# A fused attention and MLP kernel: output tiles stored as two half tiles, one slot apart

## The chip, the cores and the metric

The kernel runs on one core of a Trainium2 chip. The metric is the device time of one launch in microseconds (us). The kernel before was run three times: 504.86, 505.30 and 510.37 us, median 505.3.

## What is computed

Attention over 8 batches, 8 heads, 576 positions and head width 64, in which all scores further than tau = 0.02 below the row's maximum are dropped, followed by a two-layer network on all 4608 tokens:

```python
scores = scale * np.matmul(q, k.transpose(0, 1, 3, 2))
thresh = np.max(scores, axis=-1, keepdims=True) - tau
scores = np.where(scores >= thresh, scores, -1000000000.0)
attn = np.exp(scores - max) / (sum + 1e-09)          # row-wise
x = (attn @ v), heads side by side                    # 4608 x 512
h = x @ w_in                                          # 4608 x 2048
out = (h - np.tanh(h)) @ w_out                        # 4608 x 512
```

## The kernel before

The order of all work is written out by hand. One loop (line 852) runs over slots `s`; a slot is one score tile of 128 queries by 576 keys, and nine slots are a pair of heads. There are 288 score tiles. In each slot the program emits, in this order: the scores of a tile eight slots ahead (TensorE), their reduction to `sc` and a row maximum (VectorE, line 420), the thresholding `z` of a tile (`kink`, ScalarE, line 447), a transpose of `z`, the exponential `pT` (ScalarE), a piece of the network, finished stores, the product with v, and preparation of later pairs.

Transposes: for the first six pairs TensorE transposes `z`. For the rest `kink` issues one DMA transpose per two tiles on SyncE's queue (SP, line 454), `zT<-z`, and ScalarE's exponential (line 483) reads `zT`. `q` and `k` of the later pairs, split into two 16-bit parts on GpSimd (POOL, lines 228 to 232), are transposed by DMA on the same queue (`kT<-khl`, `qT<-qhl`, line 315); GpSimd then writes `kS` from `kT` (line 337), which TensorE needs for the scores (lines 401 and 410).

The loads of q, k and v of later pairs are issued on ScalarE's queue (`load_part`, line 175).

The network: batch after batch is taken up as a "stage" of 512 tokens as soon as its attention is done. `hidden` makes 16 tiles of 128 by 512 (psH, line 579), `bend` and `shrink` make tanh and the difference `g` (lines 592 and 598), and `project` (line 603) makes four output tiles of 128 rows by 512, each of four parts of four matmuls (psY, line 605). A stage is spread over 32 or 36 slots by a pattern of letters (`PATTERN`), so an output tile is finished every 8 to 10 slots. Stages 0 to 7 are the first 512 tokens of each batch, stage 8 the 64 left over of all batches. What is not done when the slots end runs afterwards.

An output tile is copied from PSUM to `yo` (`y_pool`, two buffers; line 617 on VectorE, or 615 on ScalarE in the tail). Its store is not issued at once: `project` appends a function to `stores`, and the slot loop runs what waits in `going` and then moves all of `stores` but the newest into `going`. So a tile's store is issued in the slot after that in which the next tile is finished. It is issued on SP, in SP's order between the transposes. The rows of a tile lie four apart in the output, 2 KB each. After the slots, all stores are issued as soon as they exist. Stage 8 stores 64 rows at a time (line 626).

Of the kernel before, what the change touches and what calls it, by code (L numbers as in the profile page):

```python
# [18 lines left out]
def kernel(  # L19
# [11 lines left out]
    nc = tc.nc  # L31
    P = 128
# [307 lines left out]
    def turn_first(t, part):  # L340

        hl = hls[0, t[0]]
        c0, c1 = ((0, 5), (5, TPP))[part]
        pl, tag = (ps_y, "y") if t == "ks" else (ps_h, "h")
        ps = pl.tile([P, 5 * P], FP16, name=f"ps1_{t}", tag=tag)
        for c in range(c0, c1):
            o = ps[:, (c - c0) * P : (c - c0 + 1) * P]
            if t == "ks":
                for a in range(2):
                    turn_chunk(o[64 * a : 64 * a + 64, :], c, hl[:, c, 1 - a, :])  # L350
            else:
                turn_chunk(o, c, hl[:, c, :, :].rearrange("p a d -> p (a d)"))
        if part == 0:
            mats[0, t] = qk_tile(t)
        dst, n = mats[0, t][:, c0 * P : c1 * P], (c1 - c0) * P
        if part == 1 or t == "q":
            nc.scalar.copy(out=dst, in_=ps[:, 0:n])
        else:
            nc.vector.tensor_copy(out=dst, in_=ps[:, 0:n])
# [17 lines left out]
    def kind(i):  # L377

        return "AB"[i % 2]

    def place(i):

        p, j = divmod(i, TPP)
        j = j - p % 2
        return (p, None, 4) if j in (-1, 8) else (p, j // 4, j % 4)

    def scores(i):
        p, hh, t = place(i)
        qT, kT, kS = mats[p, "q"], mats[p, "k"], mats[p, "ks"]
        ps = ps_big.tile([P, 1024], F32, name="psS", tag="big")  # L390
        main, rem, lo = slice(0, 512), slice(512, 576), 0
        if kind(i) == "B":
            main, rem, lo = slice(512, 1024), slice(448, 512), 448
        if hh is None:
            qrem = REM
            if q_by_dma(p):
                qrem = (slice(512, 640, 2), slice(513, 640, 2))
            for n, kk in enumerate((kT, kS)):
                for dst, cols in ((main, main_keys), (rem, rem_keys)):
                    for hh in range(2):  # L400
                        nc.tensor.matmul(  # L401
                            out=ps[64 * hh : 64 * hh + 64, dst],
                            lhsT=qT[:, qrem[hh]], rhs=cols(p, kk, hh),
                            start=(n == 0), stop=(n == 1),
                        )
        else:
            lhs = qT[:, (5 * hh + t) * P : (5 * hh + t + 1) * P]
            for n, kk in enumerate((kT, kS)):
                for dst, cols in ((main, main_keys), (rem, rem_keys)):
                    nc.tensor.matmul(  # L410
                        out=ps[:, dst], lhsT=lhs, rhs=cols(p, kk, hh),
                        start=(n == 0), stop=(n == 1),
                    )
        sc = sc_pool.tile([P, S], F32, name="sc")
        if kind(i) == "B":
            mx = mxs[i] = mxs.pop(i - 1)
        else:
            mx = mxs[i] = mx3[i // 2 % len(mx3)]
        c = int(kind(i) == "B")
        nc.vector.tensor_scalar(  # L420
            out=sc, in0=ps[:, lo : lo + S], scalar1=SC, scalar2=None,
            op0=ALU.mult, op1=ALU.max, accum_out=mx[:, c : c + 1],
        )
        scs[i] = sc

    def shift(i):

        if kind(i) == "A":
            return
        mx = mxs.pop(i)  # L430
        nb = st_pool.tile([P, 9], F32, name="nb", tag="nb")
        nc.vector.tensor_scalar(  # L432
            out=nb.rearrange("p (a b) -> p a b", b=3)[:, :, 0:2],
            in0=mx.rearrange("p (a b) -> p a b", b=4)[:, :, 0:3],
            scalar1=-1.0, scalar2=tau, op0=ALU.mult, op1=ALU.add,
        )
        nbs[i - 1], nbs[i] = nb[:, 0:1], nb[:, 1:2]
# [135 lines left out]
    gs, stores = {}, []  # L573
# [29 lines left out]
    def project(m, ms, part, ps, last, cols=slice(0, d_model)):  # L603
        for n in range(4 * part, 4 * part + 4):
            nc.tensor.matmul(  # L605
                out=ps, lhsT=gs[m][:, n, ms * P : (ms + 1) * P],
                rhs=w_out_sb[:, n, cols], start=(n == 0), stop=(n == DF_C - 1),
            )
        if part == 3:
            nc_ = cols.stop - cols.start  # L610

            pl, tag = (y_pool, "yo") if nc_ == d_model else (t_pool, "th")
            yo = pl.tile([P, d_model], F32, name="yo", tag=tag)[:, 0:nc_]
            if last:
                nc.scalar.copy(out=yo, in_=ps)
            else:
                nc.vector.tensor_copy(out=yo, in_=ps)  # L617
            if m < B:
                rows = out[m * S : m * S + MB, :].rearrange("(p c) n -> c p n", c=4)
                stores.append(lambda: nc.sync.dma_start(out=rows[ms], in_=yo))  # L620
            else:
                for h in range(2):
                    b = 2 * ms + h
                    eng = nc.scalar if h and nc_ < d_model else nc.sync
                    stores.append(
                        lambda b=b, h=h, eng=eng: eng.dma_start(
                            out=out[b * S + MB : (b + 1) * S, cols],
                            in_=yo[64 * h : 64 * h + 64, :],
                        )
                    )  # L630


    EARLY = lambda m: 3 if m else 3
# [150 lines left out]
    for p in range(DUAL, NPAIR):  # L784
        first = TPP * p - AHEAD
        at = lambda d, f: plan.setdefault(first - d, []).append(f)
# [45 lines left out]

    todo, stage = [], 0

    going = []
    fold = const.tile([P, 64], BF16, name="fold")

    for at in sorted(plan):
# [7 lines left out]
    for i in range(NTILE + 3):  # L846
        at = i - SOONER[min(i // TPP, 6)]
# [4 lines left out]
    for s in range(-AHEAD, NTILE + LAG + 3):  # L852
        p, j = divmod(max(s, 0), TPP)
        if 0 <= s < NTILE and j == 2 + LAG and p % HPAIR == 0 and p >= HPAIR:
            assert not todo
            todo = [(s + i, step) for i, step in layers(stage, False, PATTERN(stage))]
            stage += 1
        if s == NTILE:
            todo = [(s + n, step) for n, step in enumerate(layers(stage, True))]
            stage += 1  # L860
        if 0 <= s + AHEAD - 1 < NTILE:
            shift(s + AHEAD - 1)

        n = s + AHEAD
        if 0 < n < NTILE and place(n)[1] is None and kind(n) == "B":
            scores(n - 1)
        if 0 <= n < NTILE and (place(n)[1] is not None or kind(n) == "B"):
            scores(n)
        if s == 1 - AHEAD:
            for t in ("k", "q", "ks"):  # L870
                turn_first(t, 1)
        for i in kinks.pop(s, []):
            kink(i)
        bend()
        for i in wts.pop(s, []):
            weights(i)
        while todo and todo[0][0] <= s < NTILE + FIRST:
            todo.pop(0)[1]()
        if s == 0:
            nc.vector.tensor_tensor(  # L880
                out=fold, in0=ident_bf[:, 0:64], in1=ident_bf[:, 64:P], op=ALU.add
            )
        shrink()
        for store in going:
            store()
        going = stores[:-1]
        del stores[:-1]
        for i in atts.pop(s, []):
            pp, jj = divmod(i, TPP)
            if i < NTILE:  # L890
                attend(i)
                odd = pp % 2
                if jj == 3 + odd:
                    norm(pp, 0)
                elif odd and jj in (0, 8):
                    norm(pp - (jj == 0), 1)
            if pp and jj == 1 + pp % 2:
                emit_x(pp - 1)
        for step in plan.pop(s, []):
            step()  # L900
        for _ in range(cast_when.count(s + AHEAD)):
            w_cast()
        for _ in range(load_when.count(s + AHEAD)):
            w_load(next(pieces))

    for store in going:
        store()
    for _, step in todo:
        step()
        bend()  # L910
        shrink()
        for store in stores:
            store()
        stores.clear()
    while stage < NMB:
        for step in layers(stage, True):
            step()
            bend()
            shrink()
            for store in stores:  # L920
                store()
            stores.clear()
        stage += 1
# [37 lines left out]
```

## Time and profile before

| what | value |
|---|---|
| median of three runs | 505.3 us |
| profiled execution: time, span of its instructions | 511.6 us, 509.7 us |
| output tiles stored whole on SP (line 620) | 32, of 256 KB; median 3.8 us from issue to landing |
| `zT<-z` transposes on SP | 117, median 4.7 us to landing |
| `kT<-khl`, `qT<-qhl` transposes on SP | 23 and 24, median 5.2 and 4.3 us |
| 64-row stores of stage 8 (line 626) | 6 of 128 KB and 2 of 64 KB on SP, 2 of 64 KB on ScalarE's queue |

The profiled execution took 6.3 us longer than the median of the runs. Engines are PE (TensorE matmuls), PEld (its weight loads), DVE (VectorE), ACT (ScalarE), POOL (GpSimd) and SP (SyncE); a "q" behind a name means the engine's instruction queue. Issuing a DMA takes time on the queue that issues it; landing is when its data is confirmed written. In a row of slices each digit is a fortieth of the span, 9 meaning 90% or more. A line of waits reads: who waited, for what, us in total, how often, the longest. In the view of one line, the three numbers with slashes are the minimum, median and maximum duration in ns.

### The profile page before, as it was taken

Reading aid. Unit: us, or ns where it says so; the run is one execution under the profiler, and the core shown is the slowest. Engines: PE = TensorE matmul, PEld = TensorE weight load, DVE = VectorE, ACT = ScalarE, POOL = GpSimd, SP = SyncE. Lnnn points to the kernel's source line nnn. Section 1 sums busy time; section 2 is a strip of 40 time slices with the busy share of each in tenths; the row PEclk is TensorE's granted clock in tenths of the full one; section 3 lists DMA queues with packets and bytes.
Section 4 is the critical chain, followed back from the end, with each engine's and each line's share of the span. In section 5 each row is a group of like instructions: output and inputs, shape, how many; then the busy total and the mean of one; then the engine's idle time right before and its main releaser. Section 6 shows DMA issues by size and latency. Waiting matters only on the chain.

```text
span 509.7 us, 12184 instructions
## 1 busy us (share of the span) xinstructions
PE 484.8 (95%) x4283; PEld 270.9 (53%) x4345; DVE 400.2 (79%) x1150; ACT 431.7 (85%) x617; POOL 291.4 (57%) x390
## 2 busy tenths in 40 slices
PE   8999899889999989999999999999998999999997
PEld 4666566445555545555555555555554555544444
DVE  5899978878889879988898789889886887544440
ACT  5999998889999889999999999899979999533430
POOL 8999999886765375757675666569456700000000
PEclk9999999989999999999999999999999999999999
DMA  7852658999999999999999999999999986311013
GB/s 206 262 155 89 195 190 220 159 225 214 231 217 245 192 254 209 238 241 242 242 195 221 261 238 225 207 242 240 213 191 258 187 144 115 87 41 42 23 41 82
DMA packets 233341, 95.32 MB, mean 187 GB/s; under 512 B 203968, under 2 KB 222656, under 8 KB 233280
## 3 DMA queue, kind: packets, MB, share of 16 engines
q1 hardware_dynamic: 212336, 72.87, 75.1%
q10 hardware_dynamic: 20944, 21.67, 16.1%
q8 instruction: 34, 0.56, 0.5%
q14 instruction: 27, 0.22, 0.2%
HBM read 36.70 MB, written 9.44 MB: 91 GB/s over the span
## 4 chain that ended last, share of the span: by engine, by line
PE 57%; POOL 12%; DMA 9%; issue 7%; ACT 7%; DVE 5%; ACTq 1%; SPq 0%; POOLq 0%; DVEq 0%
PE psY L605 18%; PE psH L579 14%; PE psS L410 13%; DMA zT<-z 6%; PE psO L513 3%; POOL kS L337 3%; PE psHt L579 3%; ACT pT L483 3%; DMA vraw<-in_v_dram 3%; ACT z L447 2%; DVE g L598 2%; POOL qhl L232 2%; DVE sc L420 2%; PE psS L401 2%; ACTq L175 1%
## 5 line engine op out<-in xcount | busy, mean ns | idle before, releaser
L420 DVE TENSOR_SCALAR_CACHE_REDUCE sc<-psS 128x576 f32<-128x576 f32 x288 | 213.5, 752 | 27.1 <-PE psS L410 12.9
L447 ACT ACTIVATE z<-sc,nb 128x576 bf16<-128x576 f32 x288 | 216.1, 770 | 8.0 <-DVE nb L432 5.7
L483 ACT ACTIVATE pT<-zT 128x1152 f16<-128x1152 bf16 x117 | 135.2, 1155 | 12.3 <-DMA zT<-z 10.6
L605 PE MATMUL psY<-w_out_sb,g 128*128 128x512 bf16 (+1 forms) x564 | 140.8, 373 | 1.6 <-issue 0.2
L579 PE MATMUL psH<-xT,w_in_sb 128*128 128x512 bf16 x448 | 119.4, 381 | 5.1 <-issue 2.0
L337 POOL COPY kS<-kT 64x1152 f16<-64x1152 f16 x62 | 70.8, 1142 | 86.3 <-DMA kT<-khl 72.7
L598 DVE SCALAR_TENSOR_TENSOR g<-th,psH 128x512 bf16<-128x512 f32 x128 | 87.6, 685 | 33.6 <-ACT th L592 32.9
L410 PE MATMUL psS<-kT,qT 128*128 128x512 f16 (+1 forms) x512 | 104.7, 286 | 4.1 <-DVE sc L420 1.9
L410 PE MATMUL psS<-kS,qT 128*128 128x512 f16 (+1 forms) x512 | 105.1, 287 | 0.0
L410 PEld LDWEIGHTS <-qT 128*128 128x128 f16 x1024 | 72.5, 98 | 59.0 <-issue 3.8
L592 ACT ACTIVATE th<-psH 128x512 f32<-128x512 f32 x128 | 74.6, 583 | 21.4 <-PE psH L579 21.4
L605 PEld LDWEIGHTS <-g 128*128 128x128 bf16 x592 | 51.1, 98 | 54.6 <-DVE g L598 0.4
L579 PEld LDWEIGHTS <-w_in_sb 128*128 128x128 bf16 x576 | 49.4, 98 | 57.4 <-issue 6.3
L513 PE MATMUL psO<-vb,pT 128*128 128x65 bf16 x1024 | 53.3, 194 | 0.0
L513 PEld LDWEIGHTS <-pT 128*128 128x128 f16 x1024 | 44.2, 98 | 9.6
L232 POOL TENSOR_TENSOR qhl<-qraw,qhl 128x576 f16<-128x576 f32 x31 | 39.7, 1281 | 2.6
L232 POOL TENSOR_TENSOR khl<-kraw,khl 128x576 f16<-128x576 f32 x31 | 39.7, 1280 | 2.7
L475 ACT ACTIVATE pT<-psZ 128x512 f16<-128x512 bf16 (+1 forms) x54 | 35.1, 654 | 2.4 <-PE psZ L466 2.1
L506 PE MATMUL psO<-vb,pT 128*128 128x130 bf16 x128 | 28.2, 220 | 3.7 <-ACT pT L483 3.6
L617 DVE COPY yo<-psY 128x512 f32<-128x512 f32 (+1 forms) x31 | 21.1, 680 | 13.1 <-PE psY L605 12.4
L539 DVE TENSOR_TENSOR osb<-psO,rc 128x256 bf16<-128x256 f32 x64 | 27.2, 424 | 2.2
L228 POOL TENSOR_SCALAR qraw<-qraw 128x576 f32<-128x576 f32 x31 | 20.8, 671 | 11.1 <-DMA qraw<-in_q_dram 10.8
(77 smaller groups left out, 452.1 us busy)
## 6 DMA issues: line engine op xcount, KB each, us to landing
out_dram<-yo SPq DMA_DIRECT2D x32, 256.0 KB, 3.8
kraw<-in_k_dram ACTq DMA_DIRECT2D x24, 288.0 KB, 4.2
qraw<-in_q_dram ACTq DMA_DIRECT2D x24, 256.0 KB, 4.3
wt<-in_moe_w_in_dram SPq DMA_DIRECT2D x8, 512.0 KB, 4.6
wt<-in_moe_w_out_dram SPq DMA_DIRECT2D x8, 512.0 KB, 3.9
vraw<-in_v_dram ACTq DMA_DIRECT2D x24, 160.0 KB, 4.3
vraw<-in_v_dram ACTq DMA_DIRECT2D x24, 128.0 KB, 3.8
vraw<-in_v_dram SPq DMA_DIRECT2D x8, 256.0 KB, 3.6
```

Source lines behind the costliest of these rows:

```text
L232: nc.gpsimd.tensor_tensor(out=hl[:, :, 1, :], in0=x, in1=hl[:, :, 0, :], op=ALU.subtract)
L337: nc.gpsimd.tensor_copy(out=o, in_=i)
L410: nc.tensor.matmul(out=ps[:, dst], lhsT=lhs, rhs=cols(p, kk, hh), start=(n == 0), stop=(n == 1),)
L420: nc.vector.tensor_scalar(out=sc, in0=ps[:, lo : lo + S], scalar1=SC, scalar2=None, op0=ALU.mult, op1=ALU.max, accum_out=mx[:, c : c + 1],)
L447: nc.scalar.activation(out=z, in_=sc, func=ACT.Prelu, bias=nb, scale=1.0, alpha=STEEP)
L475: nc.scalar.activation(out=pt[:, off * P : (off + n) * P], in_=ps[:, 0 : n * P], func=ACT.Exp)
L483: nc.scalar.activation(out=pt[:, 0 : n * P], in_=zts.pop(i)[:, 0:n, :], func=ACT.Exp)
L513: nc.tensor.matmul(out=po[:, t - 1 + ab, :], lhsT=pt[:, blk * P : (blk + 1) * P], rhs=vb[:, hh, c, :], start=False, stop=(n == 7), skip_gr ...
L579: nc.tensor.matmul(out=ps, lhsT=w_in_sb[:, c, n * P : (n + 1) * P], rhs=xs[m][:, c, :] if m < B else xR[:, c, :, :], start=(c == 0), stop= ...
L592: nc.scalar.activation(out=th, in_=ps, func=ACT.Tanh)
L598: nc.vector.scalar_tensor_tensor(out=gs[m][:, n, :], in0=th, scalar=-1.0, in1=ps, op0=ALU.mult, op1=ALU.add,)
L605: nc.tensor.matmul(out=ps, lhsT=gs[m][:, n, ms * P : (ms + 1) * P], rhs=w_out_sb[:, n, cols], start=(n == 0), stop=(n == DF_C - 1),)
```

## The change

A whole tile's store becomes two stores of 64 rows each. `stores` now holds a list per output tile, and `going` is a dictionary from slot to stores: the first half goes to the slot in which the whole store went, the second half to the next slot. The other stores are lists of one. After the slots, whatever is left in `going` is issued in order of slot, and later tiles issue both halves together.

```diff
             if m < B:
                 rows = out[m * S : m * S + MB, :].rearrange("(p c) n -> c p n", c=4)
-                stores.append(lambda: nc.sync.dma_start(out=rows[ms], in_=yo))
+                stores.append([
+                    lambda at=at: nc.sync.dma_start(out=rows[ms, at, :], in_=yo[at, :])
+                    for at in (slice(0, 64), slice(64, P))
+                ])
...
-    going = []
+    going = {}
...
         shrink()
-        for store in going:
+        for store in going.pop(s, []):
             store()
-        going = stores[:-1]
+        for tile_stores in stores[:-1]:
+            for n, store in enumerate(tile_stores):
+                going.setdefault(s + 1 + n, []).append(store)
         del stores[:-1]
...
-    for store in going:
-        store()
+    for s in sorted(going):
+        for store in going[s]:
+            store()
     for _, step in todo:
         step()
         bend()
         shrink()
-        for store in stores:
+        for store in sum(stores, []):
             store()
         stores.clear()
```

In SP's order inside the loop, "store, zT, kT, zT, zT, qT" becomes "half, zT, half, kT, zT, zT, qT". The orders of the other engines stay as they are.

More of the change, by code (lines that the diff above doesn't have):

```diff
@@ L624, in project @@
                     eng = nc.scalar if h and nc_ < d_model else nc.sync
-                    stores.append(
+                    stores.append([
                         lambda b=b, h=h, eng=eng: eng.dma_start(
@@ L629, in project @@
                         )
-                    )
+                    ])
     EARLY = lambda m: 3 if m else 3
@@ L919 @@
             shrink()
-            for store in stores:
+            for store in sum(stores, []):
                 store()
```

## The prediction

> **What bounds the kernel now.** I first read the page of the profiled execution: the engines' busy shares and the slices.
>
> ```profile
> PE 484.8 (95%) x4283; PEld 270.9 (53%) x4345; DVE 400.2 (79%) x1150; ACT 431.7 (85%) x617; POOL 291.4 (57%) x390
> ...
> DMA  7852658999999999999999999999999986311013
> ```
>
> TensorE is the bound; the DMA engines are full from about 90 to 400 us. So I cut the span at the places where the DMA row changes and asked for the busy time of each stretch (PE, PEld, DVE, ACT, POOL, clock, DMA share, GB/s):
>
> ```profile
> 160.00:395.00 235.00, 228.31 (x2022) 125.23 (x2056) 202.44 (x599) 222.53 (x304) 149.27 (x188) 1.00 1.20 228
> 395.00:436.00 41.00, 39.95 (x335) 21.74 (x340) 33.03 (x95) 37.81 (x53) 8.95 (x12) 1.00 0.84 146
> 436.00:510.00 74.00, 69.82 (x361) 33.55 (x365) 29.55 (x48) 25.52 (x42) 0.00 (x0) 1.00 0.17 51
> ```
>
> In the crowded stretch TensorE loses only 235.0 - 228.3 = 6.7 us. In 13 us windows most stretches show 12.8 to 12.9 us of TensorE; three lose more: 172 to 185 (11.72), 328 to 341 (12.19) and 380 to 393 (10.90). The waits of that stretch say what comes late:
>
> ```profile
> POOL kS L337 <- DMA kT<-khl: 64.9, 16, 7.9
> ...
> ACT pT L483 <- DMA zT<-z: 8.8, 10, 2.2
> ```
>
> ScalarE waits 8.8 us for transposed tiles zT. GpSimd waits far longer for kT, but TensorE's wait for the kS made from it is 0.4 us, once in the whole span: GpSimd's wait costs nothing. The stores share SP's queue with these transposes, so the timeline of SP matters (start, us, instruction); here around the first loss:
>
> ```profile
> 166.40 0.62 SPq L620 DMA_DIRECT2D out_dram<-yo  x1
> 167.12 1.31 SPq L454 DMA_TRANSPOSE zT<-z  x1
> 168.53 1.89 SPq L315 DMA_TRANSPOSE kT<-khl  x1
> 170.51 6.57 SPq L454 DMA_TRANSPOSE zT<-z  x2
> 177.18 1.26 SPq L315 DMA_TRANSPOSE qT<-qhl  x1
> ```
>
> SP goes from one issue to the next in about 0.1 us. From 140 to 400 us its issues take 228.6 us of the 260; what is left beyond 0.1 us each is 18.4 us. But the 125 transposes issued there take 216.5 us, 1.73 each, though one alone takes 1.25 to 1.3 (the seven from 414 to 434 us take 1.24 to 1.30). The excess, 216.5 - 125 x 1.28 = 56.5 us, I read as SP held up by full rings: the DMA engines, not SP, set the pace. Landing agrees: 3.2 to 3.3 us for most of the uncrowded zT after 405 us, up to 8.6 in the stretch.
>
> I then set zT's landing against the start of the exponential that reads it, by place behind the store. The 20 tiles directly behind it take 5.38 us to land; ScalarE waits 2.0 us for them in all. The first zT behind kT is the tight one: also 5.38 us, at most 0.1 us to spare in 9 of 19, and 6.9 us of ScalarE's waits. Later ones have 1 to 3 us to spare in most periods.
>
> **What the Trainium skill says.** "DMA: Bandwidth & Descriptors", section "Queues, rings and completion order": what a sequencer issues goes on its own row of rings and each DMA engine consumes its ring in order. So a store of SP stands ahead of SP's next transposes; the trace fits, since zT directly behind a store lands 0.5 us later than zT at the fourth and sixth places (5.38 against 4.92 and 4.86). The same page, section "Rules for kernel authors", says of two transfers to disjoint partition halves "Don't bother — they serialize": both run on the same 16 engines. The trace of before has no such pair of tiles to show it, but its 128 KB stores of 64 rows (line 626) land in 2.4 us and its 256 KB stores of the uncrowded tail in 2.1: half the bytes save nothing.
>
> **The change part by part.**
>
> ```profile
> L620 SPq DMA_DIRECT2D out_dram<-yo x32: 332/530/1509, 140.0 to 490.7; - x32
> L626 SPq DMA_DIRECT2D out_dram<-yo x8: 466/516/1074, 496.4 to 506.6; - x8
> ```
>
> These are the issue times (min/median/max ns) of the whole stores and of the existing 64-row stores.
>
> *Issues.* 32 stores become 64. Compute instructions, their order and all bytes stay. In SP's order 22 whole stores stand inside the slot loop. The change separates the halves of 19 of them by one zT; of the last three in the loop and the ten after it both halves follow one another. A half issues like line 626, 0.52 us (332 ns at least, as in the tail), plus 0.1 to the next: 0.62. In the crowded stretch that is 19 x 0.62 = 11.8 us more of SP.
>
> *What stands behind it.* The period was store, zT, kT, zT, zT, qT, ...; it becomes half, zT, half, kT, zT, zT, qT. The second half delays kT and the tight zT by up to 0.62 us. kT and that zT already exceed 1.28 us by 0.65 and 0.68 (means 1.93 and 1.96): if this is waiting for ring space, the half's issue uses time in which SP would have stood still, the engines meanwhile have about 2 us of queued work (5.4 us landing against 3.3), and the tight zT lands when the same bytes ahead of it are done. Bounds: nothing, and 0.62 in each of the 9 tight places, 5.6 us of ScalarE. I take a third, 0.2 x 9 = 1.8 us. From 172 to 185 TensorE lost 13.0 - 11.72 - 0.15 (its usual shortfall) = 1.1 us while ScalarE waited about 2.6: under half. So +0.8 us.
>
> *The first zT.* Half the store now stands ahead of it. 256 KB at the stretch's 228 GB/s is 1.15 us, so 0.57 less. Of its 2.0 us of ScalarE's waits (three tiles) at most 1.7 goes, at TensorE some 0.7; as the bytes only move to kT and the next zT, I take -0.3. Bounds 0 and -0.7.
>
> *kT later.* kS on GpSimd starts later by the same up to 0.62 us. It is a constant shift, not a growing one, and GpSimd is busy 149 of 235 us. Cost nothing; the cover is the time between kS and its first use. If it failed, "psS waits for kS" would appear.
>
> *Buffer yo.* Two buffers; the copy on VectorE two tiles later needs both halves landed. In the crowded stretch the store had landed 4.3 to 10.5 us ahead of that copy, and 2.3 us at the loop's end (store at 434.8). The second half is issued about 0.1 + 1.52 + 0.1 = 1.7 us after the first half's issue ends: at least 2 us remain. At the loop's end no transpose parts them, which takes 0.6 off 2.3. Nothing. Otherwise VectorE would stop with the scores' reductions queued behind the copy.
>
> *After the loop.* Ten second halves, 0.33 to 0.52 us each. SP waits there for yo (33.8 us behind VectorE, 18.1 behind ScalarE), one tile lasts 6.5 us, and DMA share is 0.17. The very last stores, of line 626, are untouched. Nothing.
>
> Sum: 0.8 - 0.3 = **+0.5 us** on the profiled execution, 511.6 us (span 509.7 and 1.9 around it), so 512.1. The median of the runs shown is 505.3, 6.3 lower; I put the same difference on it: 505.8, and give **506**.
>
> **The rivals.**
>
> *SP itself decides (slower).* The excess in the issue times is not waiting for rings but the transposes' own cost beside other traffic. Then every inserted half pushes kT and all zT behind it, until a gap in SP; only 18.4 us of gaps exist, hardly any from 359 to 390 us, where the worst loss is. With 0.62 on each of the 9 tight tiles at full price: +5.6, about 511; with all 19 periods, +11.8, 517. It decides from where SP has no gap and transposes issue in 1.3 us. For it: three of the losses begin just behind a store. Against it: issue times up to 3.84 us, which no lone transpose shows.
>
> *The burst decides (faster).* The losses start with a whole store ahead of a zT: 6.9 us landing at 167.1, 7.5 at 262.7, 7.6 at 370.2. If 128 KB less there lets each recover, most of the 6.7 us that TensorE loses could go: -3 to -5, about 501. Against: the second half returns two places later, ahead of the tightest tile.
>
> *It doesn't do what it says.* In 13 of 32 tiles the halves are not apart. All lie where nothing is crowded, so they neither help nor harm: 505.3.
>
> **How the numbers follow.** About no change (forecast, and the rival of no effect): 0.72, with 503.5 to 509 of its own. Slower by SP's issue: 0.22, 510.4 to 517. Burst: 0.06. One per cent, 5 us, is about what a measurement of this kernel can tell from no change; the three runs shown reach from 504.9 to 510.4 by themselves. The range takes in the whole likeliest case, part of the faster one and the lower part of the slower: 503 to 511.5. Faster by over 1% 0.06, within 0.72, slower 0.22.
>
> **What would show it.** Right: 64 stores on SP, the second half about 0.5 us; kT's and the next zT's issue times fall by about what the half takes; zT's waits at ScalarE stay near 9 us, TensorE near 228 us of the same stretch. Wrong towards slower: the same issue times as now, zT's waits rising by 5 us or more, mostly at the first zT behind kT; or VectorE's copy waiting for out_dram<-yo. Wrong towards faster: zT behind the first half landing 0.5 us sooner and the three TensorE losses gone.

## The result, and the profile after

| | before | changed |
|---|---|---|
| median of four runs each | 506.6 us (504.9 to 510.4) | 513.9 us (510.6 to 514.6) |
| ratio, 95% interval | | 1.0127 [1.0081, 1.0173] |
| profiled execution: time, span | 511.6, 509.7 us | 513.4, 511.6 us |

The change makes the kernel slower, by 1.3%. (A ratio is worked out from the single runs; it is not the quotient of the two medians.) Measured once more (e5 below) beside 43 runs of the kernel before (median 509.2 us), it was 515.8 us, 1.0153 [1.0106, 1.02]. The profiled executions of before, and of e2, e6, e8 and e12 below, were slow ones of their kernels, so the two spans understate the difference. A better reading of the traces is the time from the first copy of an output tile (line 617) to the 24th, which is the crowded stretch: 126.56 to 431.56 us before, 123.18 to 433.40 us after, 305.0 against 310.2 us, and 313.2 us in the repeat. Before entered this stretch 3.4 us later than after did, when no output tile had yet been stored. What follows the stretch takes 78.2 us in all three: the tail is untouched.

The page after, busy shares and DMA slices:

```profile
PE 490.4 (96%) x4345; PEld 271.4 (53%) x4345; DVE 399.1 (78%) x1150; ACT 431.2 (84%) x617; POOL 291.5 (57%) x390
...
DMA  7852658999999999999999999999999977411113
```

Busy PE went up, which is no sign of more work: the trace of before lacks 62 matmul records (4283 against 4345). For the same reason the 6.7 us that the prediction gives as TensorE's loss are too many. Its "usual shortfall" of 0.15 us in 13 us, which the trace after does not have, makes some 2.7 us of them, so about 4 us is an estimate of the true loss. The trace after, which is complete, shows 235.00 - 229.19 = 5.8 us between 160 and 395 us:

```profile
160.00:395.00 235.00, 229.19 (x2033) 123.94 (x2032) 199.63 (x593) 220.05 (x301) 147.16 (x185) 1.00 1.20 225
395.00:436.00 41.00, 40.65 (x351) 21.99 (x350) 33.38 (x97) 38.44 (x54) 11.12 (x16) 1.00 0.87 153
```

The waits after, between 160 and 395 us (us in all, times, longest):

```profile
POOL kS L337 <- DMA kT<-khl: 56.4, 14, 5.4
...
ACT pT L483 <- DMA zT<-z: 11.9, 10, 2.7
```

ScalarE's waits for zT grew from 8.8 to 11.9 us here; over the whole span the page's sum went from 10.6 to 15.3. They moved, too. Between 140 and 400 us, place by place as in the prediction: zT behind the first half lands in 4.83 us instead of 5.38 and nobody waits for it (2.0 us before); the first zT behind kT makes ScalarE wait 14.5 us instead of 6.9, and has at most 0.1 us to spare in 12 of 19 periods instead of 9. The repeat's trace confirms the growth, but not this division: there zT behind the first half lands in 5.24 us with 5.0 us of waits, the first zT behind kT makes 8.8 us, and the sum of all places is 14.3 us, beside 15.7 in the first trace and 10.4 before.

SP after, from 331 to 348 us (start, us, instruction):

```profile
331.53 1.74 SPq L454 DMA_TRANSPOSE zT<-z  x1
333.32 0.60 SPq L621 DMA_DIRECT2D out_dram<-yo  x1
334.03 1.33 SPq L315 DMA_TRANSPOSE kT<-khl  x1
335.45 4.47 SPq L454 DMA_TRANSPOSE zT<-z  x2
340.02 2.70 SPq L315 DMA_TRANSPOSE qT<-qhl  x1
```

Every issue follows the last one at once. The first zT of the 4.47 us lands 7.7 us after its issue and ScalarE stands 2.7 us. The view of single lines shows what the issues cost (ns, min/median/max); the last line is that of before:

```profile
L621 SPq DMA_DIRECT2D out_dram<-yo x64: 466/588/2005, 137.7 to 493.1; - x64
...
L454 SPq DMA_TRANSPOSE zT<-z x117: 1242/1494/3451, 81.4 to 435.3; - x117
```

```profile
L454 SPq DMA_TRANSPOSE zT<-z x117: 1242/1470/3841, 81.3 to 433.4; - x117
```

A half costs no less than a whole store did (median 530 ns), and the issue of zT, 1470 ns before, has not become shorter. By place, between 140 and 400 us: kT's issue fell from 1.93 us on average to 1.56 (1.76 in the repeat), but that of the zT behind it rose from 1.96 to 2.11 (2.21).

### The profile page after: what moved, and what is told of

It is laid out like the page before. It is cut to its first block, busy times and chain, and to the rows that moved or that the text cites. A ratio compares the mean times of both kernels' runs of the same rounds, so it can differ in the third digit from the quotient of the medians.

```text
span 511.6 us, 12256 instructions
## 1 busy us (share of the span) xinstructions
PE 490.4 (96%) x4345; PEld 271.4 (53%) x4345; DVE 399.1 (78%) x1150; ACT 431.2 (84%) x617; POOL 291.5 (57%) x390
## 4 chain that ended last, share of the span: by engine, by line
PE 46%; DMA 16%; POOL 13%; ACT 10%; issue 8%; DVE 4%; ACTq 2%; SPq 0%; POOLq 0%; DVEq 0%
PE psY L605 15%; PE psH L579 11%; DMA zT<-z 11%; PE psS L410 9%; ACT pT L483 4%; ACT z L447 4%; PE psHt L579 3%; DMA qraw<-in_q_dram 2%; POOL kS L337 2%; PE psO L513 2%; ACT th L592 2%; ACTq L175 2%; DMA kraw<-in_k_dram 2%; POOL qhl L232 2%; DVE g L598 2%
## 5 line engine op out<-in xcount | busy, mean ns | idle before, releaser
L483 ACT ACTIVATE pT<-zT 128x1152 f16<-128x1152 bf16 x117 | 135.1, 1155 | 17.0 <-DMA zT<-z 15.3
L605 PE MATMUL psY<-w_out_sb,g 128*128 128x512 bf16 (+1 forms) x592 | 145.7, 373 | 0.0
L579 PE MATMUL psH<-xT,w_in_sb 128*128 128x512 bf16 x480 | 123.3, 379 | 3.7 <-DVE g L598 3.5
## 6 DMA issues: line engine op xcount, KB each, us to landing
wt<-in_moe_w_in_dram SPq DMA_DIRECT2D x8, 512.0 KB, 4.6
wt<-in_moe_w_out_dram SPq DMA_DIRECT2D x8, 512.0 KB, 4.2
```

The source lines that it names most:

```text
L483: nc.scalar.activation(out=pt[:, 0 : n * P], in_=zts.pop(i)[:, 0:n, :], func=ACT.Exp)
L579: nc.tensor.matmul(out=ps, lhsT=w_in_sb[:, c, n * P : (n + 1) * P], rhs=xs[m][:, c, :] if m < B else xR[:, c, :, :], start=(c == 0), stop= ...
L605: nc.tensor.matmul(out=ps, lhsT=gs[m][:, n, ms * P : (ms + 1) * P], rhs=w_out_sb[:, n, cols], start=(n == 0), stop=(n == DF_C - 1),)
```

## The experiments

Several theories are told apart. "Issue": one more instruction on SP costs, because SP has no time to spare. "Bytes", or "place": 128 KB directly ahead of kT make kT and the next zT late. A third: splitting costs in the DMA engines, whoever issues and wherever. Ratios are to the kernel before, run beside each group; when two ratios are compared, both intervals count. The time that was left on SP is in one table behind the experiments.

**Both halves in one slot** (e1).

```diff
-                going.setdefault(s + 1 + n, []).append(store)
+                going.setdefault(s + 1, []).append(store)
```

> Both halves in the slot in which the whole store stood: half, half, zT, kT, zT. Theory 'issue' (SP has no spare time up to the first zT behind kT, so a second issue of some 0.6 us anywhere ahead of it makes it late): nearly as slow as the change, ratio to before 1.008 to 1.014, waits of ScalarE for zT 13 to 16 us. Theory 'bytes' (128 KB moved to directly ahead of kT make kT and that zT land late): bytes stand where they stood before, ratio 0.997 to 1.003, waits 9 to 11 us.

Measured: 515.9 us, 1.0179 [1.0121, 1.0238], more than either theory had expected. The bytes' place alone is not the cause. In its trace zT directly behind the halves now makes ScalarE wait (4.5 us) besides the one behind kT (7.3 us): both issues stand ahead of both.

**The whole store in the second half's place** (e2, and again as e6), so one issue per tile:

```diff
-                going.setdefault(s + 1 + n, []).append(store)
+                going.setdefault(s + 2, []).append(store)
```

> The whole store, one issue, moved to the place of the second half: zT, store, kT, zT. Theory 'issue': the number of issues ahead of the first zT behind kT is that of before, ratio 0.997 to 1.004. Theory 'bytes': all 256 KB now directly ahead of kT, slower than the change, ratio 1.015 to 1.025, most of ScalarE's waits at the first zT behind kT.

The first time six runs gave a median of 519.0 us (508.0 to 520.8) and no interval, so it was repeated.

> The whole store in the second half's place again, for an interval. Theory 'issue' alone: under 1.004. Theory 'bytes' (or both together): 1.013 to 1.025, more than the change, since 256 KB instead of 128 KB stand directly ahead of kT.

Measured: 515.3 us, 1.0104 [1.0037, 1.0171]. It falls between the two expected ranges. Without any second issue the move of the store by one place costs about 1%: the place counts too. It is not clearly worse than the change, as "bytes" alone would have it. The waits between 140 and 400 us in the repeat's profiled execution, which took 518.7 us:

```profile
ACT pT L483 <- DMA zT<-z: 16.6, 15, 2.9
```

By place, with every wait ahead of these exponentials counted (19.2 us), 15.2 us are at the first zT behind kT. As this execution took 3.4 us more than the median, the sums may be too high.

**A second issue without the bytes** (e3). The store stays whole and in its old place; the second place gets a load of 4 KB that nothing reads.

```diff
+    probe = const.tile([64, 16], F32, name="probe")
...
                 stores.append([
-                    lambda at=at: nc.sync.dma_start(out=rows[ms, at, :], in_=yo[at, :])
-                    for at in (slice(0, 64), slice(64, P))
+                    lambda: nc.sync.dma_start(out=rows[ms], in_=yo),
+                    lambda: nc.sync.dma_start(out=probe, in_=moe_w_out[0:64, 0:16]),
                 ])
```

> The whole store as before, and in the place of the second half a load of 64 rows by 64 bytes into a tile that nothing reads (adds work that the output doesn't need): one more issue with next to no bytes. Theory 'issue': ratio 1.008 to 1.014, and 6 to 8 us more of ScalarE's waits for zT. Theory 'bytes': 0.998 to 1.003.

Measured: 513.8 us, 1.0086 [1.0047, 1.0126]. The issue costs even with next to no bytes. Its view in that trace:

```profile
L622 SPq DMA_DIRECT2D probe<-in_moe_w_out_dram x24: 471/613/1762, 139.4 to 438.6; - x24
```

For 4 KB SP is held as long as for half a tile. A rival is the DMA engines' own work on the load's short rows. The trace's DMA packets speak against it: between 140 and 400 us the 64-byte packets took 13 ns each, 1.0 us of each of the 16 engines in all, while the kernel became over 4 us longer. What the load adds is thus SP's time and one more transfer in SP's queue; no run parts these two. The rise of the waits was smaller than expected: 13.5 us between 140 and 410 us, from 8.8.

**The small load behind the first zT behind kT** (e12): `s + 1 + n` becomes `s + 1 + 3 * n`.

> The whole store in the place of before, and the small load of 64 rows by 64 bytes (work that the output doesn't need) now behind the first zT behind kT: store, zT, kT, zT, small load, zT, qT. Theory 'a second issue costs only ahead of the tight zT': 0.997 to 1.004. Theory 'SP's time counts everywhere': 1.006 to 1.012, as with the load ahead of kT (1.0086).

Measured: 513.7 us, 1.0101 [1.0062, 1.014]. An added issue costs as much behind the tight tile as ahead of it, so it doesn't act through that one tile alone.

**Stores at other places.** For e4, e7, e8, e10, e17 and e18 a tile's store no longer waits for the next tile to be finished, but is issued a fixed number of slots after its own:

```diff
-        for tile_stores in stores[:-1]:
+        for tile_stores in stores:
             for n, store in enumerate(tile_stores):
-                going.setdefault(s + 1 + n, []).append(store)
-        del stores[:-1]
+                going.setdefault(s + 4, []).append(store)
+        stores.clear()
```

Two halves, `s + 4 + 2 * n` (e4: kT, zT, half, zT, half, qT):

> Two halves as in the change, but four and six slots after the tile is finished, both behind the first zT behind kT: kT, zT, half, zT, half, qT. Theories 'issue' and 'bytes' alike, as nothing stands ahead of the tight zT any more: as fast as before or faster, 0.988 to 1.000, and ScalarE's waits at that zT under 6 us. A third theory, that a second store in the ring between transposes costs wherever it stands: 1.008 to 1.014.

Measured: 512.0 us, 1.0054 [1.0015, 1.0094], between the two ranges. The first zT behind kT no longer waits at all (0.0 us), but the others do (13.0 us): the cost has moved on.

The whole store, `s + 4` (e7: kT, zT, store, zT, qT):

> The whole store, one issue, four slots after its tile is finished: kT, zT, store, zT, qT. Theory 'what stands directly ahead of kT and its zT costs': better than before, 0.985 to 0.998, waits at the first zT behind kT under 5 us. Theory 'the DMA engines are full and any place costs the same': 0.997 to 1.004.

Measured: 504.4 us, 0.9935 [0.9907, 0.9963], faster than both kernels. Its stretch from 160 to 395 us, and its waits between 140 and 400 us:

```profile
160.00:395.00 235.00, 234.68 (x2100) 127.52 (x2099) 207.00 (x611) 227.20 (x310) 154.01 (x195) 1.00 1.20 232
```

```profile
ACT pT L483 <- DMA zT<-z: 1.4, 2, 1.2
```

TensorE loses 0.3 us of 235. The same bytes by the same number of issues, at another place, make 1% worse than before (e6) or 0.65% better.

The whole store, `s + 6` (e8: kT, zT, zT, store, qT):

> The whole store, one issue, six slots after its tile is finished: kT, zT, zT, store, qT. Theory 'place': 0.985 to 0.998, like four slots. Theory 'any place costs the same': 0.997 to 1.004. Against the two halves of four and six slots (1.0054) it tells what the second issue costs away from kT: 0.004 to 0.010 if SP's issue time counts everywhere, nothing if it counts only ahead of the tight zT.

Measured: 509.3 us, 1.0001 [0.9969, 1.0033]. That is what "any place costs the same" had, and "place" missed: not every place behind the tight tile is good. The two halves of e4 stand at the places of e7 and e8, one at each. They are slower than e7, and than e8 by 0.005, with intervals that overlap.

Both halves at `s + 4` (e10):

> Both 64-row halves one after the other, four slots after the tile is finished: kT, zT, half, half, zT, qT. Beside the whole store at that place (0.9935) it gives the price of the split where the place is good. Theory 'a second issue costs wherever it stands': 0.999 to 1.004. Theory 'it costs only ahead of the tight zT': 0.990 to 0.997.

Measured: 511.7 us, 1.0072 [1.0039, 1.0105], against 0.9935 for the whole store there. The split costs 1.4% at the best place tried too, more than either theory had.

The whole store at `s + 4`, followed at once by the small load (e17):

> The whole store behind the first zT behind kT (0.9935 alone), followed at once by the small load of 64 rows by 64 bytes (work that the output doesn't need). If the second issue on SP makes two halves there slower (1.0072): 1.001 to 1.008. If it is the shape of the halves: 0.992 to 0.997.

Measured: 507.1 us, 1.0032 [1.0011, 1.0053]. The second issue with next to no bytes takes back 1.0032 - 0.9935 = 1.0%.

**Halves by columns.** Each half is `rows[ms][:, at]` from `yo[:, at]` with `at` 256 columns wide, in the places of the change (e9) and both at `s + 4` (e18).

> Two halves in the places of the change, but cut by columns (128 rows by 256, 1 KB a row) instead of by rows: every half touches all 128 partitions. If the second issue and its place make the cost, as slow as the change: 1.009 to 1.018. If reading 64 partitions alone makes a half slow in the DMA engines (a 2 KB row took 125 ns in the change's trace, 102 in that of before), clearly less: 1.000 to 1.009.

> Two halves cut by columns (128 rows by 256) one after the other behind the first zT behind kT. If the second issue makes the cost: 1.001 to 1.009, like halves of 64 rows. If the 64 partitions do: 0.992 to 0.998.

Measured: e9 513.0 us, 1.0125 [1.0082, 1.0168]; e18 507.9 us, 1.0016 [0.9989, 1.0043]. In the change's places columns are no better than rows. At the good place they cost what the small load costs, and less than halves of 64 rows (1.0072); the intervals barely overlap. Whether 64 rows add something of their own stays open.

**The issue taken from SP.** The change with its second half on GpSimd's queue (e11), and the whole store there at `s + 7` (e15) and `s + 4` (e16):

```diff
-                    lambda at=at: nc.sync.dma_start(out=rows[ms, at, :], in_=yo[at, :])
-                    for at in (slice(0, 64), slice(64, P))
+                    lambda at=at, eng=eng: eng.dma_start(out=rows[ms, at, :], in_=yo[at, :])
+                    for at, eng in ((slice(0, 64), nc.sync), (slice(64, P), nc.gpsimd))
```

> The change with the second half issued on GpSimd's queue (it stands there ahead of the split of k), so SP issues as often as before. If SP's second issue and the bytes in SP's ring ahead of kT make the cost: 0.996 to 1.005. If the split costs through the DMA engines whoever issues it, or GpSimd's issue makes the split of k late: 1.008 to 1.018.

> The whole store issued on GpSimd's queue behind the split of q, seven slots after its tile is finished; in the tail on SP as before. SP issues one store per tile less, the bytes stay. If SP's issue is what counts: 0.985 to 0.995. If the bytes count and go by any queue: 0.997 to 1.004. If GpSimd's issue makes kS or the split late: above 1.004, with waits of kT for GpSimd.

> The same four slots after the tile is finished, between the split of k and that of q. As the run before it; if it is slower by over 0.005, the place of the bytes in time counts although no transposes stand behind them in the same ring.

Measured: e11 511.2 us, 1.0043 [1.0011, 1.0074]; e15 509.3 us, 1.0026 [0.9997, 1.0056]; e16 511.2 us, 1.009 [1.0053, 1.0128]. Taking the second half off SP removes about two thirds of the change's cost; its bytes leave SP's queue with it, so this run by itself does not part issue and bytes. But a whole store off SP is no gain: one issue fewer, and the expectation of 0.985 to 0.995 missed. The bytes still run beside the transposes, whose issues take 1.81 and 1.86 us in these traces. Why they grew is open. And e16 is slower than e15 by 0.006, more than the 0.005 that was set for it. That reads as the bytes' place in time counting even off SP's queue; that GpSimd's own issue at that place costs something is not excluded.

**The store's bytes taken away, then its issue.** e13 stores a corner of 64 rows by 64 bytes at the place of before; e14, with `[:0]` in place of `[:1]`, issues no store in the loop. After the loop both store whole tiles.

```diff
+                    lambda: nc.sync.dma_start(out=rows[ms, 0:64, 0:16], in_=yo[0:64, 0:16]),
+                    lambda: nc.sync.dma_start(out=rows[ms], in_=yo),
...
-            for n, store in enumerate(tile_stores):
+            for n, store in enumerate(tile_stores[:1]):
```

> In the slot loop each store of 256 KB is replaced by one of 64 rows by 64 bytes at the same place: 22 output tiles are left out but for that corner. If SP's issue alone counts: 0.997 to 1.003. If the bytes in the DMA engines count: 0.980 to 0.993, and the mean issue time of the transposes between 140 and 400 us falls from 1.73 us to 1.6 or less.

> No store at all in the slot loop (22 output tiles are left out). Against the run before it, one issue per tile less: if SP's time is what bounds the crowded stretch, 0.006 to 0.012 lower than that run; if not, the same as that run.

Measured: 503.7 us, 0.9943 [0.9924, 0.9962], and 502.8 us, 0.9927 [0.9904, 0.9949]. All that the loop's stores cost the kernel before is thus about 0.7%, and e7 with all its bytes can't be told from no store at all. The first step is the bytes', if just short of the expected range: with nearly the same issues as before, the transposes' mean fell from 1.73 to 1.58 us. The second step, the issue alone, is 0.0016, within the intervals: with the bytes gone one issue per tile costs nothing that can be told. The stretch of the kernel without stores:

```profile
160.00:395.00 235.00, 234.94 (x2090) 127.31 (x2088) 207.29 (x611) 227.40 (x311) 154.25 (x197) 1.00 1.16 212
```

**SP's account.** Between 140 and 400 us, from the traces: what SP's issues took, and what was left between them beyond the 0.1 us that each needs. The traces of e2, e6, e8 and e12 are not in it.

| kernel | transposes: number, us, mean | other issues: number, us | left, us | ratio |
|---|---|---|---|---|
| no store (e14) | 128, 195.6, 1.53 | 0, 0 | 52.5 | 0.9927 |
| 4 KB stores (e13) | 127, 201.1, 1.58 | 19, 11.6 | 32.4 | 0.9943 |
| whole behind tight zT (e7) | 128, 209.2, 1.63 | 20, 12.1 | 25.2 | 0.9935 |
| before | 125, 216.5, 1.73 | 20, 12.1 | 18.4 | 1 |
| e7's place, by columns (e18) | 125, 210.7, 1.69 | 40, 21.7 | 12.1 | 1.0016 |
| before + small load (e3) | 123, 209.6, 1.70 | 37, 27.1 | 8.5 | 1.0086 |
| halves past (e4) | 122, 208.3, 1.71 | 38, 28.9 | 7.2 | 1.0054 |
| e7 + small load (e17) | 125, 215.3, 1.72 | 40, 23.1 | 6.6 | 1.0032 |
| the change | 123, 212.2, 1.73 | 36, 26.8 | 6.5 | 1.0127 |
| the change, by columns (e9) | 123, 214.7, 1.75 | 38, 23.5 | 6.0 | 1.0125 |
| halves together (e1) | 122, 217.8, 1.78 | 38, 23.2 | 4.4 | 1.0179 |
| e7's place, halves (e10) | 124, 216.7, 1.75 | 40, 24.3 | 4.1 | 1.0072 |
| the change again (e5) | 124, 214.5, 1.73 | 38, 28.5 | 2.4 | 1.0153 |
| second half on GpSimd (e11) | 125, 220.8, 1.77 | 19, 15.9 | 9.3 | 1.0043 |
| whole on GpSimd (e15) | 126, 228.0, 1.81 | 0, 0 | 21.0 | 1.0026 |
| whole on GpSimd (e16) | 123, 229.3, 1.86 | 0, 0 | 18.8 | 1.009 |

> The change itself once more, beside the same runs of before as the next three: 1.009 to 1.017. Its first zT behind kT makes ScalarE wait 12 to 16 us.

(The repeat's waits at the first zT behind kT were 8.8 us, fewer than expected; zT at other places made up 5.5 us.)

Where SP issues the stores, the kernels with more left on SP are by and large the faster ones, with place as a second factor. The last two rows don't fit: e16 has as much left as before and is 0.9% slower. So what is left on SP is a sign of the price and not all of it. The change puts 14.7 us of issues more into these 260 us; 11.9 us come out of what was left and the rest shows as two transposes fewer: the kernel is behind.

Where the time is left matters as much. Of the 18.4 us of before, only 1.8 stand ahead of kT or the first zT behind it; 14.7 stand ahead of zT that follow another zT, where SP waits for ScalarE's next `z`. The change puts its second half directly ahead of kT, and in both its traces nothing is left from there to the first zT behind kT.

The cost can be set beside parts measured alone: the issue, 0.86% (e3), and half of the move, 0.5 x 1.04% (e6), are 1.4%, beside 1.3 and 1.5 measured. That this is more than chance is not shown, for e1 is off the sum: it has the issue and no move, and costs 1.8%. Why it costs more than the change is open.

## Why the prediction was wrong

- **What bounds the kernel.** The transposes' path, and within it the first zT behind kT, was the right place to look: its wait grew from 6.9 to 14.5 us, and to 8.8 in the repeat. That TensorE fills the stretch when zT comes in time is confirmed by e7 and e14. The 6.7 us of TensorE's loss were read too high, by some 2.7 us of missing records; the three stretches named there do lose.
- **Issues.** 64 stores, 19 pairs parted: as worked out. A half's issue was put at 0.52 us; between 140 and 400 us it measured 0.75 on average.
- **The step that failed is "What stands behind it"**: that "the half's issue uses time in which SP would have stood still", by which a third of 0.62 us at nine places, +0.8 us at TensorE, was left. The change measured 1.3%, more than 6 us. The prediction's own sign for this step was that the issue times of kT and the next zT fall by what the half takes, 0.75 us. kT's did fall, by 0.37 us (0.17 in the repeat), but the next zT's rose by 0.15 (0.25): together they fell by 0.2 us in one trace and rose by 0.1 in the other. The mean of all transposes stayed at 1.73 us in both. So the half's time was not hidden in their excess; most of it came out of the gaps on SP, and next to none of these lay where the half was put. The reading behind the step was half right: without the store's bytes the transposes' issues do get shorter (1.58 us in e13, 1.53 in e14), but they don't get shorter, on the whole, because SP comes later.
- **A second error of the same step:** nine tight places were counted as the only ones at which a delay matters. e12 and e4 show that an issue costs behind the tight zT too. The rival "SP itself decides" came nearest: it said that an inserted half pushes what stands behind it until a gap in SP, and its two prices, 5.6 us for nine tight places and 11.8 for all 19 periods, lie on either side of what was measured. The argument against it (issues of up to 3.84 us) did not bear on it. It is not the whole either: e6 and e16 cost about 1% without any added issue on SP.
- **The first zT.** Half the store less ahead of it: 0.55 us sooner in the first trace, 0.57 predicted, and its waits gone; but 0.14 us sooner in the repeat, with 5.0 us of waits. So the gain of this term is not shown. That the bytes come back at kT was said, but not priced; e6 prices the whole move at 1.0%. The rival "The burst decides" did not come true: what gained was moving the bytes past the tight tile (e7), not cutting them.
- **kT, yo, the tail.** GpSimd's wait for kT went from 64.9 to 56.4 us, and to 68.1 in the repeat, and neither trace lists a wait of TensorE for kS; no wait of the copy on a store is listed; the tail took 78.2 us before and after. All as predicted. Making the store issue earlier (e7) also left `yo` alone.

## What to carry to other kernels

A queue that issues DMAs has a time budget like an engine: add up its issue times over the crowded stretch, and count an added issue at full price against the gaps that are left near its place, even where the other issues look stretched by waiting. Cutting a transfer in two buys a smaller burst with a second issue; here, moving the whole transfer directly behind the instruction with least to spare got the gain without the price. One transpose further on the gain was gone (e8), so such a place has to be tried. Removing the work altogether (e14) tells cheaply how much there is to gain at all.

## What the runs showed of the hardware

- A store of half the rows, or a load of 4 KB, holds SP about as long as a store of 256 KB: median 588 ns, 613 (477 in e17) and 530 ns.
- Where a plain store stands among the transposes of the same queue matters: the same whole store gave 0.9935 directly behind the first zT behind kT, 1.0001 one transpose later, and 1.0104 directly ahead of kT.
- The section "Rules for kernel authors" of the Trainium skill's page "DMA: Bandwidth & Descriptors" advises against two transfers to disjoint partition halves because they share the same engines. These runs agree with the advice: between 140 and 400 us a half of the change landed 4.0 us after its issue on average (4.1 in the repeat), a whole store before 4.35, so half the bytes saved little. They add a price that the section does not name: the change cost 1.3 to 1.5%, and one more issue with next to no bytes 0.9 to 1.0%.
- That page says in "Issuing engines are not separate DMA queues" that another issuing engine only saves the sequencer's time, "usually small relative to the DMA itself". Here that time mattered: with the second half on GpSimd's queue the ratio was 1.0043, with both halves on SP 1.0127 and 1.0153. The sentence before it, that DMAs run on the same 16 engines whoever starts them, fits: whole stores on that queue did not get out of the transposes' way (1.0026 and 1.009).
